# Attention output with tokens on partitions: the state's part on two row groups, masked scores as full weights

## The chip, the cores and the metric

The kernel runs on one core of a Trainium2 chip. The metric is the device time of one execution in microseconds, the median over several runs. A ratio is the mean time of one kernel's fast runs over the mean time of the other's fast runs of the same rounds, so it is not quite the ratio of the medians that are quoted.

## The reference

A block-wise linear attention ("lightning attention") is followed by a mixer. There are 4 batches, 8 heads, 768 tokens and 64 channels per head; all is float32.

```python
for b in range(nb):                                   # blocks along the tokens
    intra = einsum('bhic,bhjc->bhij', qb, kb) * Dmask
    intra = einsum('bhij,bhjd->bhid', intra, vb)
    inter = einsum('bhid,bhde->bhie', qb * lam_pow, kv_state)
    out[:, :, sl] = intra + inter
    kv_state = lam_block * kv_state + einsum('bhsd,bhse->bhde', kb * rev_pow, vb)
# x = out as (batch, token, head*channel)
u  = x + (x^T @ U @ V)^T                              # low rank over the tokens, rank 32
out = u + relu(u @ w_ch1) @ w_ch2                     # 512 -> 2048 -> 512
```

The kernel uses blocks of 128 tokens, 6 per batch, so it goes through 24 blocks (`s` = 0 to 23), each for all 8 heads. Head `h = 2a + x` has `a` from 0 to 3 and `x` 0 or 1; `x` chooses the upper or the lower 64 partitions.

## The kernel before

Only the attention front is concerned. In each block, q and k are transposed (`prep`), the scores are formed and masked, and the output comes out with *channels* on partitions: v and the state are the weights, the masked scores and the queries are moved through. It is then transposed back.

```python
kv  = consts.tile([P, HP, P], FP32)      # state of two heads, block-diagonal, zeros between
kvc = consts.tile([P, HP, D], FP32)      # the same without the zeros

def outputs(s):
    px = bank([P, HP, P], "px", "a2")
    for a in range(HP):
        if c > 0:
            for x in range(2):
                rows = slice(x * D, (x + 1) * D)
                nc.tensor.matmul(out=px[rows, a, :], lhsT=kv[:, a, rows], rhs=qs[:, a, :], ...)   # L359
        for x in range(2):
            nc.tensor.matmul(out=px[x*D:(x+1)*D, a, :], lhsT=vr[:, 2*a+x, :], rhs=sm[:, x, a, :], ...)  # L364
    nc.scalar.copy(xt, px)
    state(s)

def state(s):                            # pkv = (scaled k)^T v, 8 matmuls, L380
    for a in range(HP):
        nc.vector.scalar_tensor_tensor(kvc[:, a, :], kvc[:, a, :], lamc[:, a, :], pkv[:, a, :], ALU.mult, ALU.add)
    for x in range(2):                   # into the block-diagonal form
        nc.scalar.copy(kv[d, :, d], kvc[d])

def back(s):                             # four transposes, L404
    for ct in range(CT):
        nc.tensor.transpose(out=px[:, ct, :], in_=xt[:, ct, :], identity=ident)
    nc.scalar.copy(xs[s]..., px)
```

Later steps of a block are `mix` (adds the low-rank part to x), `turn` (transposes x for the first large product), and "side work": pieces of the conversion of U, V and the first weights, spread over the blocks.

## Time and profile before

| | before |
|---|---|
| median | 699.68 us (698.73 to 700.88, 4 runs) |
| span of the profiled run | 697.5 us |
| attention front, up to the first large product | 142.2 us |
| time per steady block | 5.67 us |

A steady block is one with everything in it: state, mix and turn. I measure a block from the start of its scores to the start of the next scores. The groups that the change touches, in the first 155 us (columns: line, engine, operation, output and inputs, shapes, count; busy us and mean ns of one; idle time before them):

```profile
L364 PE MATMUL px<-sm,vraw 128*64 128x128 f32 x384 | 35.4, 274 | 0.4 <-DVE x_nat L450 0.3
L359 PE MATMUL px<-qs,kv 128*64 128x128 f32 x320 | 32.1, 279 | 0.0
L364 PEld LDWEIGHTS px<-sm,vraw 128*64 128x64 f32 x384 | 23.6, 137 | 1.9 <-DVE x_nat L450 1.4 <-issue 0.4 <-DVE sm L347 0.2
L404 PE MATMUL pxn<-ident,xt 128*128 128x128 f32 x96 | 15.7, 286 | 0.4 <-ACT xt L369 0.4
```

`128*64 128x128` is a matmul with 128 rows and 64 columns of weights and 128 moving columns. The 384 instructions of L364 are 24 blocks x 8 heads x 2, because each float32 product stands in the trace as two instructions, each with its own weight load. The mean of 274 ns is one instruction's latency. Many overlap, so pace must be read from the chain, not from the mean.

### The profile page before, as it was taken

What the parts mean: (1) busy time and instruction counts of PE and PEld (TensorE: products, weight loads), DVE (VectorE), ACT (ScalarE), POOL (GpSimd) and SP (SyncE); (2) the same over time, 40 slices, a digit from 0 to 9 for tenths busy, and PEclk for the clock granted to TensorE, in tenths of its full rate; (3) what the DMA queues carried; (4) which work ended last, traced back from release to release, by engine and by line L of the source; (5) the groups of instructions that cost most, each with busy time, mean ns of one, the idle gap of its engine ahead of it and who ended that gap; (6) DMA issues with size and microseconds to landing.
All of it is one profiled execution on the core that took longest, in us unless ns stands there. A gap on an engine that the chain in (4) does not pass through costs nothing.

```text
span 697.5 us, 11418 instructions
## 1 busy us (share of the span) xinstructions
PE 685.6 (98%) x4194; PEld 556.0 (80%) x4194; DVE 502.0 (72%) x905; ACT 306.6 (44%) x543; POOL 108.0 (15%) x91
## 2 busy tenths in 40 slices
PE   7999999998999999999999999999999999999997
PEld 6879797976888888888888888888888888888886
DVE  5768687867899777777779436778577586775864
ACT  4767777844566544444455322232232222322320
POOL 4425554523000000000000000011030030300300
PEclk9999999999999999999999999999999999999999
DMA  9977686224476565556557889966344363352521
GB/s 219 228 182 183 167 221 163 90 81 168 173 256 245 197 210 210 208 209 208 205 206 266 296 304 359 341 206 200 98 153 155 91 211 103 120 185 91 166 92 60
DMA packets 131530, 131.17 MB, mean 188 GB/s; under 512 B 81234, under 2 KB 89426, under 8 KB 131474
## 3 DMA queue, kind: packets, MB, share of 16 engines
q1 hardware_dynamic: 129376, 129.92, 57.8%
q10 hardware_dynamic: 2098, 0.52, 0.3%
q8 instruction: 33, 0.54, 0.3%
q14 instruction: 23, 0.19, 0.1%
HBM read 80.09 MB, written 50.33 MB: 187 GB/s over the span
## 4 chain that ended last, share of the span: by engine, by line
PE 93%; DVE 4%; issue 1%; ACT 1%; DMA 1%; ACTq 0%; DVEq 0%
PE pz L638 25%; PE pz L771 13%; PE pz L769 13%; PE pd L773 13%; PE pd L648 12%; PE pss L341 3%; PE px L364 3%; PE px L359 2%; PE pxn L404 2%; PE pkv L380 2%; PE put L464 1%; PE pk L306 1%; PE pq L306 1%; DVE ut L469 1%; DVE sm L347 1%; PE pr L433 1%
## 5 line engine op out<-in xcount | busy, mean ns | idle before, releaser
L638 PE MATMUL pz<-u_hl,w 128*128 128x512 f32 x768 | 190.6, 398 | 1.1 <-ACT uf L476 1.1
L638 PEld LDWEIGHTS pz<-u_hl,w 128*128 128x128 f32 x768 | 144.4, 188 | 37.1 <-ACT uf L476 1.5
L771 PE MATMUL pz<-w_hl,m 128*128 128x512 f32 x384 | 151.6, 396 | 0.0
L769 PE MATMUL pz<-w_hl,m 128*128 128x512 f32 x384 | 151.6, 396 | 0.0
L773 PE MATMUL pd<-w_d,m 128*128 128x512 f32 x384 | 150.0, 396 | 0.0
L752 ACT ACTIVATE m<-mt 128x512 fp32r<-128x512 f32 x96 | 60.7, 632 | 196.8 <-PE pd L773 137.0
L753 DVE SCALAR_TENSOR_TENSOR m<-rm,m 128x512 fp32r<-128x512 f32 x96 | 71.5, 746 | 52.3 <-ACT m L752 52.1
L653 DVE SCALAR_TENSOR_TENSOR r<-pd,r 128x512 f32<-128x512 f32 x96 | 61.8, 686 | 57.2 <-ACT r L644 47.2
L793 POOL TENSOR_TENSOR o<-o,u 128x512 f32<-128x512 f32 x20 | 29.8, 1522 | 452.1 <-DVE o L791 452.1
L648 PE MATMUL pd<-u_d,w 128*128 128x512 f32 x384 | 98.8, 397 | 0.0
L769 PEld LDWEIGHTS pz<-w_hl,m 128*128 128x128 f32 x384 | 72.3, 188 | 17.7
L771 PEld LDWEIGHTS pz<-w_hl,m 128*128 128x128 f32 x384 | 72.3, 188 | 17.6
L773 PEld LDWEIGHTS pd<-w_d,m 128*128 128x128 f32 x384 | 72.3, 188 | 17.6
L648 PEld LDWEIGHTS pd<-u_d,w 128*128 128x128 f32 x384 | 72.2, 188 | 17.4
L644 ACT ACTIVATE r<-pz 128x512 f32<-128x512 f32 x96 | 51.9, 593 | 62.4 <-PE pz L638 62.4
L754 DVE SCALAR_TENSOR_TENSOR m<-m 128x512 fp32r<-128x512 f32 x96 | 69.1, 721 | 0.9
L751 DVE TENSOR_SCALAR mt<-rm 128x512 uint32<-128x512 uint32 x96 | 46.2, 482 | 28.2 <-DMA rm<-r_d 27.6
L347 DVE TENSOR_TENSOR sm<-pss,mask 128x512 f32<-128x512 f32 x48 | 30.9, 686 | 11.5 <-PE pss L341 9.3
L179 ACT CAST w<-wt 128x512 fp32r<-128x512 f32 x32 | 19.9, 622 | 41.8 <-DVE wt L176 33.5
L364 PE MATMUL px<-sm,vraw 128*64 128x128 f32 x384 | 35.4, 274 | 0.4 <-DVE x_nat L450 0.3
L359 PE MATMUL px<-qs,kv 128*64 128x128 f32 x320 | 32.1, 279 | 0.0
L136 ACT ACTIVATE sc<-sc,ends 128x512 f32<-128x512 uint32 x29 | 21.0, 723 | 19.2 <-DVE sc L132 19.2
(88 smaller groups left out, 761.9 us busy)
## 6 DMA issues: line engine op xcount, KB each, us to landing
r_d<-r SPq DMA_DIRECT2D x96, 256.0 KB, 2.7
rm<-r_d SPq DMA_DIRECT2D x96, 256.0 KB, 2.6
words<-in_moe_w_ch_dram SPq DMA_DIRECT2D x32, 512.0 KB, 4.4
w_d<-w SPq DMA_DIRECT2D x16, 768.0 KB, 3.3
w_hl<-w_d SPq DMA_DIRECT2D x16, 512.0 KB, 6.0
u_d<-x_nat SPq DMA_DIRECT2D x24, 256.0 KB, 3.0
u<-u_d SPq DMA_DIRECT2D x24, 256.0 KB, 4.3
out_dram<-o SPq DMA_DIRECT2D x24, 256.0 KB, 2.0
```

The lines of the kernel that those rows point to most:

```text
L364: nc.tensor.matmul(out=px[x * D : (x + 1) * D, a, :], lhsT=vr[:, 2 * a + x, :], rhs=sm[:, x, a, :], start=(c == 0), stop=True,)
L638: nc.tensor.matmul(out=acc[g][0], lhsT=w[:, n, ct, :], rhs=uhl[g][:, n, ct, :], start=(ct == 0 and n == 0), stop=(ct == CT - 1 and n == 1),)
L644: nc.scalar.mul(rs[g], acc[g][0], 1.0 + E)
L648: nc.tensor.matmul(out=acc[g][1], lhsT=w[:, 2, ct, :], rhs=ud[g][:, ct, :], start=(ct == 0), stop=(ct == CT - 1),)
L653: nc.vector.scalar_tensor_tensor(rs[g], acc[g][1], 4096.0, rs[g], ALU.mult, ALU.add)
L751: nc.vector.tensor_scalar(t.bitcast(U32), r.bitcast(U32), HI, None, ALU.bitwise_and)
L752: nc.scalar.activation(out=m[:, 0], in_=t, func=AF.Relu)
L753: nc.vector.scalar_tensor_tensor(m[:, 1], r, 0.0, hi, ALU.max, ALU.subtract)
L754: nc.vector.scalar_tensor_tensor(m[:, 2], hi, E, low, ALU.mult, ALU.subtract)
L769: nc.tensor.matmul(out=pz, lhsT=m[:, 0, cols], rhs=hl[:, 0], start=first, stop=False)
L771: nc.tensor.matmul(out=pz, lhsT=m[:, 1, cols], rhs=hl[:, 1], start=False, stop=end)
L773: nc.tensor.matmul(out=pd, lhsT=m[:, 2, cols], rhs=dd, start=first, stop=end)
```

## The change

It intends to get x straight with *tokens* on partitions, so that the transposes back and a copy go away. For that the roles are swapped: queries and masked scores become the weights, the state and v move. The state's part uses two row groups (64 rows each), so the state needs no zero blocks; its fading by lambda goes to ScalarE; PSUM is laid out anew for the front, with pairs of banks for scores and output; the order of the steps is changed.

```diff
-    kv = consts.tile([P, HP, P], FP32, name="kv")
-    kvc = consts.tile([P, HP, D], FP32, name="kvc")
+    def fade(s):
+        if 0 < s % NT < NT - 1:
+            for a in range(HP):
+                nc.scalar.mul(faded[:, a, :], kv[s][:, a, :], lamc[:, a, :])
     def state(s):
+            if c == 0:
+                nc.vector.tensor_copy(out=kv[s + 1], in_=pkv)
+            else:
+                nc.vector.tensor_tensor(out=kv[s + 1], in0=pkv, in1=st[s]["faded"], op=ALU.add)
-    def back(s): ...            # four transposes and the loop of outputs(s) go
+    def inter(s):
+        for a in range(HP):
+            for x in range(2):
+                nc.tensor.matmul(
+                    out=px[:, x, a, :], lhsT=st[s]["qs"][half[x], a, :], rhs=kv[s][half[x], a, :],
+                    start=(a == 0), stop=False,
+                )
+    def intra(s):
+        for a in range(HP):
+            for x in range(2):
+                nc.tensor.matmul(
+                    out=px[:, x, a, :], lhsT=sm[:, x, a, :], rhs=vr[:, 2 * a + x, :],
+                    start=first, stop=(first or a == HP - 1),
+                )
+        nc.scalar.copy(xs[s].rearrange("p (a x e) -> p x a e", a=HP, x=2), px)
...
-        step += [("scale", s + 1)] + [("aside", s)] + [("mix", done)] + [("low", b - 1)]
-        step += [("outputs", s)] + [("low_sum", b - 1)] + [("scores", s + 1), ("back", s)] + [("turn", done)]
+        step = [("prep", s + 1), ("fade", s), ("scale", s + 1)] + [("mix", done)] + [("low", b - 1)]
+        step += [("intra", s)] + [("turned", done - 1)] + [("aside", s)] + [("low_sum", b - 1)]
+        step += [("state", s)] + [("scores", s + 1), ("inter", s + 1)] + [("turn", done)]
+    pieces += [("mix", NS - NT - 1)]      # the last mix of the front, before: at the head of the first product's list
```

More of the change, by code (lines that the diff above doesn't have):

```diff
@@ L210, with two_banks, one_bank @@
     words_pool.append(att_ctx.enter_context(tc.tile_pool(name="words_a", bufs=1)))
-    ps = ctx.enter_context(tc.tile_pool(name="ps", bufs=8, space=bass.MemoryType.PSUM))
+    front_ctx = ctx.enter_context(ExitStack())
+    psf = front_ctx.enter_context(tc.tile_pool(name="psf", bufs=1, space=bass.MemoryType.PSUM))
+    def two_banks(name, tag):
+        return psf.tile([P, 2, N], FP32, tag=tag, name=name)
+    def one_bank(shape, name, tag):
+        return psf.tile(shape, FP32, tag=tag, name=name)
+    psa = []
     def bank(shape, name, tag):
-        return ps.tile(shape, FP32, tag=tag, bufs=2, name=name)
+        return psa[0].tile(shape, FP32, tag=tag, bufs=2, name=name)
     lamb = consts.tile([P, H], FP32, name="lamb")
@@ L272, in constants @@
         nc.vector.tensor_copy(out=rev, in_=mask[:, :, :, P - 1])
-        nc.gpsimd.memset(kv, 0.0)
     def powers():
@@ L297 @@
     st = {}
+    kv = {}
+    half = [slice(0, D), slice(D, P)]
     def prep(s):
@@ L302, in prep @@
         for a0 in range(0, HP, n):
-            for name, dst in (("q", qt), ("k", kt)):
-                pt = bank([P, n, P], "p" + name, "b2")
+            for name, dst, tag in (("q", qt, "pt" if a0 else "pq"), ("k", kt, "pu" if a0 else "pk")):
+                pt = one_bank([P, n, P], "p" + name, tag)
                 for a in range(a0, a0 + n):
@@ L332, in scale @@
             scale_k(s + 1)
+    def fade(s):
+        if 0 < s % NT < NT - 1:
+            st[s]["faded"] = faded = att.tile([P, HP, D], FP32, tag="faded", name="faded")
+            for a in range(HP):
+                nc.scalar.mul(faded[:, a, :], kv[s][:, a, :], lamc[:, a, :])
     def scores(s):
         qt, kt = st[s]["qt"], st[s]["kt"]
-        pss = [bank([P, HP, P], "pss", "a1") for x in range(2)]
+        pss = two_banks("pss", "pss").rearrange("p x (a i) -> p x a i", a=HP)
         for a in range(HP):
             for x in range(2):
-                rows = slice(x * D, (x + 1) * D)
                 nc.tensor.matmul(
-                    out=pss[x][:, a, :], lhsT=kt[rows, a, :], rhs=qt[rows, a, :],
+                    out=pss[:, x, a, :], lhsT=kt[half[x], a, :], rhs=qt[half[x], a, :],
                     start=True, stop=True,
@@ L346, in scores @@
         for x in range(2):
-            nc.vector.tensor_tensor(out=sm[:, x], in0=pss[x], in1=mask[:, x], op=ALU.mult)
+            nc.vector.tensor_tensor(out=sm[:, x], in0=pss[:, x], in1=mask[:, x], op=ALU.mult)
         st[s]["sm"] = sm
-    def outputs(s):
-        b, c = divmod(s, NT)
-        qs, sm, vr = st[s].get("qs"), st[s]["sm"], raw[s, "v"]
-        px = bank([P, HP, P], "px", "a2")
-        for a in range(HP):
-            if c > 0:
-                for x in range(2):
-                    rows = slice(x * D, (x + 1) * D)
-                    nc.tensor.matmul(
-                        out=px[rows, a, :], lhsT=kv[:, a, rows], rhs=qs[:, a, :],
-                        start=True, stop=False,
-                    )
-            for x in range(2):
-                nc.tensor.matmul(
-                    out=px[x * D : (x + 1) * D, a, :], lhsT=vr[:, 2 * a + x, :],
-                    rhs=sm[:, x, a, :], start=(c == 0), stop=True,
-                )
-        xt = att.tile([P, HP, P], FP32, tag="xt", bufs=1, name="xt")
-        nc.scalar.copy(xt, px)
-        state(s)
-        st[s] = xt
     def state(s):
-        b, c = divmod(s, NT)
+        c = s % NT
         if c < NT - 1:
             ks, vr = st[s]["ks"], raw[s, "v"]
-            pkv = bank([P, HP, D], "pkv", "a2")
+            pkv = one_bank([P, HP, D], "pkv", "pu")
             for a in range(HP):
@@ L380, in state @@
                     nc.tensor.matmul(
-                        out=pkv[x * D : (x + 1) * D, a, :], lhsT=ks[:, a, x, :],
-                        rhs=vr[:, 2 * a + x, :], start=True, stop=True,
-                    )
-            for a in range(HP):
-                if c == 0:
-                    if a == 0:
-                        nc.vector.tensor_copy(out=kvc, in_=pkv)
-                else:
-                    nc.vector.scalar_tensor_tensor(
-                        kvc[:, a, :], kvc[:, a, :], lamc[:, a, :], pkv[:, a, :],
-                        ALU.mult, ALU.add,
-                    )
@@ L393, in state @@
-            for x in range(2):
-                d = slice(x * D, (x + 1) * D)
-                nc.scalar.copy(kv[d, :, d], kvc[d])
+                        out=pkv[half[x], a, :], lhsT=ks[:, a, x, :], rhs=vr[:, 2 * a + x, :],
+                        start=True, stop=True,
+                    )
+            kv[s + 1] = att.tile([P, HP, D], FP32, tag="kv", bufs=2, name="kv")
+            if c == 0:
+                nc.vector.tensor_copy(out=kv[s + 1], in_=pkv)
+            else:
+                nc.vector.tensor_tensor(out=kv[s + 1], in0=pkv, in1=st[s]["faded"], op=ALU.add)
@@ L396, in state @@
+        del st[s]
         del raw[s, "v"]
         load_next("v")
-    def back(s):
-        xt = st.pop(s)
-        px = bank([P, CT, P], "pxn", "b1")
-        for ct in range(CT):
-            nc.tensor.transpose(out=px[:, ct, :], in_=xt[:, ct, :], identity=ident)
+    def inter(s):
+        st[s]["px"] = both = two_banks("px", "px")
+        px = both[:, :, 0 : HP * D].rearrange("p x (a e) -> p x a e", a=HP)
+        if s % NT == 0:
+            return
+        for a in range(HP):
[4 more added lines that the diff above has]
+                )
@@ L405, in back @@
+    def intra(s):
+        first = s % NT == 0
+        sm, vr, px = st[s]["sm"], raw[s, "v"], st[s]["px"]
+        px = px[:, :, 0 : HP * D].rearrange("p x (a e) -> p x a e", a=HP)
+        for a in range(HP):
[4 more added lines that the diff above has]
+                )
         xs[s] = x_pool.tile([P, C], FP32, tag="x", name="x_nat")
-        nc.scalar.copy(xs[s].rearrange("p (c n) -> p c n", n=P), px)
+        nc.scalar.copy(xs[s].rearrange("p (a x e) -> p x a e", a=HP, x=2), px)
@@ L409 @@
     pts = {}
     def low(b):
-        pp = bank([P, C], "pp", "a2" if b < B - 1 else "b2")
+        pp = two_banks("pp", "pss")[:, 0] if b < B - 1 else bank([P, C], "pp", "b2")
         for c in range(G):
@@ L418, in low @@
             )
-        half = C // 2
+        n = C // 2
         assert 2 * (NT - G) == G
         for i in range(G):
-            c, cols = G + i // 2, slice(i % 2 * half, (i % 2 + 1) * half)
+            c, cols = G + i // 2, slice(i % 2 * n, (i % 2 + 1) * n)
             nc.tensor.matmul(
@@ L431, in low_sum @@
     def low_sum(b):
-        pr = bank([P, C], "pr", "b1" if b < B - 1 else "b2")
+        pr = one_bank([P, C], "pr", "pt") if b < B - 1 else bank([P, C], "pr", "b2")
         nc.tensor.matmul(
@@ L445, in mix @@
         b, c = divmod(s, NT)
-        pu = bank([P, C], "pu", "a2" if s < NS - NT - 1 else "b2")
+        pu = one_bank([P, C], "pu", "pu") if s < NS - NT else bank([P, C], "pu", "b2")
         nc.tensor.matmul(
@@ L461, in turn @@
         cols = slice(n * P, (n + 1) * P)
-        pt = bank([P, CT, P], "put", "b1")
+        pt = one_bank([P, CT, P], "put", "pt") if g < FG else bank([P, CT, P], "put", "b1")
         for ct in range(CT):
@@ L488, in turn @@
         turned[s] = rest
-    pieces = [("prep", 0), ("scale", 0), ("scores", 0)]
+    pieces = [("prep", 0), ("scale", 0), ("scores", 0), ("inter", 0)]
     for s in range(NS):
@@ L497 @@
         done = s - NT - 1
-        step = [("prep", s + 1)] * (s + 1 < NS)
-        step += [("turned", done - 1)] * (done > 0)
-        step += [("scale", s + 1)] * (s + 1 < NS)
-        step += [("aside", s)]
+        more = s + 1 < NS
+        step = [("prep", s + 1)] * more + [("fade", s), ("scale", s + 1)] * more
         step += [("mix", done)] * (done >= 0)
         step += [("low", b - 1)] * (c == 0 and b > 0)
-        step += [("outputs", s)]
+        step += [("intra", s)] + [("turned", done - 1)] * (done > 0) + [("aside", s)]
         step += [("low_sum", b - 1)] * (c == 0 and b > 0)
-        step += [("scores", s + 1), ("back", s)] * (s + 1 < NS)
+        step += [("state", s)] + [("scores", s + 1), ("inter", s + 1)] * more
         step += [("turn", done)] * (done >= 0 and done // TG < FG)
         pieces += step
+    pieces += [("mix", NS - NT - 1)]
     waiting = {name: list(range(NS)) for name in "qkv"}
@@ L516 @@
     run = {
-        "prep": prep, "scores": scores, "outputs": outputs, "back": back,
+        "prep": prep, "fade": fade, "scores": scores, "inter": inter, "intra": intra,
+        "state": state,
         "low": low, "low_sum": low_sum, "mix": mix, "turn": turn,
@@ L591 @@
     make_gather()
-    pl = bank([P, H], "pl", "a2")
+    pl = one_bank([P, H], "pl", "pu")
     nc.tensor.matmul(out=pl, lhsT=lam_row[:, H:], rhs=lam_row[:, 0:H], start=True, stop=True)
@@ L596 @@
     scale_k(0)
+    powers()
     run["aside"] = aside
@@ L599 @@
         run[what](s)
-        if (what, s) == ("scores", 0):
-            powers()
     assert not side
+    front_ctx.close()
+    psa.append(
+        ctx.enter_context(
+            tc.tile_pool(name="ps", bufs=2, space=bass.MemoryType.PSUM, reuse_waits="tile")
+        )
+    )
     def enter_first_product(s):
@@ L692 @@
     rest = [
-        (0, 0, "mix", c0 - 1), (0, 4, "back", NS - 1), (0, 4, "enter", None),
+        (0, 4, "enter", None),
         (0, 4, "turn", c0 - 2), (0, 9, "low", b), (0, 14, "low_sum", b),
```

## The prediction

> **What bounds the kernel now.** I read the page first (busy shares and the chain that ended last), then the table of windows, the chain of one steady attention block, the groups of instructions, and single rows of the timeline. The page:
>
> ```profile
> PE 685.6 (98%) x4194; PEld 556.0 (80%) x4194; DVE 502.0 (72%) x905; ACT 306.6 (44%) x543; POOL 108.0 (15%) x91
> ...
> PE 93%; DVE 4%; issue 1%; ACT 1%; DMA 1%; ACTq 0%; DVEq 0%
> PE pz L638 25%; PE pz L771 13%; PE pz L769 13%; PE pd L773 13%; PE pd L648 12%; PE pss L341 3%; PE px L364 3%; PE px L359 2%; PE pxn L404 2%; PE pkv L380 2%; PE put L464 1%; PE pk L306 1%; PE pq L306 1%; DVE ut L469 1%; DVE sm L347 1%; PE pr L433 1%
> ```
>
> TensorE carries 93% of the chain. Three quarters of the span (the products of lines 638 to 773) are not touched. Only the attention front, about the first 142 us, changes. There, too, TensorE hardly rests, while VectorE and ScalarE are busy about 75% (columns: stretch, length, then busy us and count for PE, PEld, DVE, ACT, POOL, then clock, DMA share, GB/s):
>
> ```profile
> 80.00:100.00 20.00, 19.81 (x270) 17.59 (x270) 16.80 (x37) 16.10 (x31) 9.55 (x8) 1.00 0.74 194
> 100.00:120.00 20.00, 19.66 (x261) 16.05 (x259) 14.91 (x28) 14.49 (x28) 9.70 (x9) 1.00 0.72 180
> ```
>
> Busy time alone could hide waits, so I took one steady block from the chain (start, us, work):
>
> ```profile
> 90.03 0.56 PE pkv L380 x16
> 90.59 1.09 PE pss L341 x16
> 91.68 0.59 PE pxn L404 x4
> 92.27 0.44 PE put L464 x4
> 92.70 0.44 PE pq L306 x4
> 93.14 0.44 PE pk L306 x4
> 93.58 0.23 PE pu L447
> 93.81 0.37 PE px L359 x4
> 94.18 0.22 PE px L364 x4
> 94.39 0.22 PE px L359 x4
> ...
> 95.70 0.63 PE pkv L380 x16
> ```
>
> The block lasts 95.70 - 90.03 = 5.67 us and every piece of it is TensorE. So freed work on VectorE or ScalarE is worth nothing here; what counts is whether TensorE's own list of work gets longer or shorter. The chain shows 4.91 us for each early block (no residual mix, no turning yet) and 71.26 to 84.91 for two blocks, one of which carries the low-rank sums: those contain VectorE pieces, but the timeline has TensorE idle for only some 0.6 us before px there, so there is little waiting to win back.
>
> **What the Trainium skill says, and whether the trace agrees.** (1) "TensorE: Matmul & The Clock Gate", section "LDWEIGHTS (loading the stationary operand)": a weight load takes its number of columns / 1.2 ns, whatever the number of rows: 107 ns for 128 columns, 53 for 64. The trace agrees where two full fp32 loads stand back to back:
>
> ```profile
> 77.69 0.30 PEld L433 LDWEIGHTS pr<-pt,gather 128*128 128x128 f32 x2
> 77.69 1.12 PE L433 MATMUL pr<-pt,gather 128*128 128x512 f32 x2
> ```
>
> One load lasts 188 ns (its mean in the groups), two end after 0.30 us, so the second began some 0.11 us after the first. (2) "TensorEngine Tiling (Array Packing)", "Key Properties": tiles run in parallel, and changing the tiling mode drains the engine. The trace agrees: in px, four instructions on two column tiles take 0.22 us, a pair per 0.109, while the first four after the switch take 0.37. (3) The same page, "Gotcha 1: PSUM Pressure": row tiles write different banks; the change gives x two banks, as the scores have already. (4) "ScalarE: Activation LUTs", "What ACT_TABLE_LOAD costs": an activation is 186 ns + 0.833 ns per element, 93 more for a per-partition operand. The 64x256 copy kv should then take 399 ns; the trace has 404.
>
> What sets a matmul's pace in this kernel: each fp32 product is two instructions[...]. A group streams at the larger of its weight load (columns x 0.84 ns) and its moving side (128 columns per 109 ns, from the transposes: 0.44 us for four), since loads run ahead of running matmuls. pkv: 64 against 64 columns on two column tiles, 0.56 us for eight pairs. px: 64 weight columns against 128 moving, eight pairs 0.88 us. pss: 128 against 128 on two row tiles, 1.09 with the fill, 0.112 per pair.
>
> **The change part by part**, in a steady block.
> - The transposes back go: pxn, -0.59 us of TensorE, and one ScalarE copy of 0.58 (xt). x is then written by one strided copy of 0.6, as now.
> - px from state and queries (L359) becomes "inter": queries are the weights, 64 rows x 128 columns, on two row tiles; the state moves, 64 columns. The moving side halves, but the weight side doubles, so the load sets the pace as in pss: 8 pairs x 0.112 = 0.90 us, against 8 x 0.109 = 0.87 now. It follows pss in the same mode, so no drain between. About even: the zeros that are left out gave nothing, because the two column tiles already ran side by side.
> - px from masked scores and v (L364) becomes "intra": 128x128 weights with 64 moving columns, no tiling. Before: 8 pairs x 0.109 = 0.87. After: 16 single instructions, one after the other, each paced by a 128-column load: 16 x 0.109 = 1.75 us. This is +0.88, more than the transposes give back.
> - Fill and drain: px's first-four excess of 0.15 goes; inter's end before put and intra's end before pkv add 0.05 and 0.10. About even.
> - VectorE: four kvc updates of 276 ns (1.10) become one 128x256 add, some 0.42 as the copy kvc<-pkv takes: -0.68, off the path. ScalarE: two kv copies (0.81) and xt (0.58) go; four fades come, each 280 + 53 = 333 ns by the skill's formula, 0.24 apart, 1.0 in all: -0.4, off the path.
>
> New steady block: pkv 0.56 + pss 1.09 + inter 0.90 + put 0.49 + pq 0.44 + pk 0.44 + pu 0.23 + intra 1.85 = 6.00, against 5.67: +0.33.
>
> Over the front of 24 blocks: nine steady ones x 0.33 = 3.0; three that follow a low-rank block (5.8 to 6.1 now, with waits, 6.0 after) +0.2; the four early ones 4.91 less pxn 0.59 and px 1.85, plus 0.90 and 1.85 and a pkv that no longer starts in px's mode (0.1): +0.4 each, 1.6; the last of a batch, no state update, two x 0.3 = 0.6; the one at 31 us loses 0.1, since its wait for the side work (VectorE vt, 1.3 us, ahead of ScalarE xt) falls away when side work moves behind intra; the three with low-rank sums have no inter and lose their waits, -0.15 together; the very first has no pxn to lose, +0.8. Sum 5.95. At the end the moved mix (VectorE add 0.68 and its latencies) holds the bank that the first product wants: +0.8, an estimate; the last transposes back (0.44) go, but the last inter and intra cost as much more. So 699.8 + 6 = some 706 us.
>
> **The rivals.**
> (a) The matmul is bound by what moves, not by loads, as the change's author may think: intra would be 16 x 0.055 = 0.87, inter 0.45; a block loses 0.59 + 0.45, some 24 us in all, 676 to 680. Against: pr's loads 0.11 apart; nothing in the trace has a 128-column load with 64 moving columns, so it isn't directly seen.
> (b) Load and stream don't overlap on the full array: intra 16 x (0.107 + 0.055) = 2.6 us, +0.85 a block, 725 us. Against: put and pq run four 128-column transposes at 0.109 each with their loads inside, and the untouched fp32r products have 188 ns loads under a 233 ns pace. But their moving side is the longer one; a switch cost of 10 to 17 ns per instruction when the load is the longer is possible and adds up to 6 us (712).
> (c) New waits: x's two banks, pkv, put's bank have one buffer each now. inter(s+1) needs the x copy of s (intra's end + 0.8; pkv and pss give 1.65) and the state's add (pkv's end + 0.6, pss gives 1.0). VectorE's list per block is then some 4.6 us of 6.0. These fit, except in the low-rank blocks (VectorE has 5.9 us there), where a few tenths could be lost: 707 to 709.
> (d) The shorter dependency saves hidden waits: at most the 0.2 to 0.4 us of the eight irregular blocks, 2 to 3 us: 703.
>
> **Range and chances.** The centre is 706. (c), (d) and a switch cost give -4 to +6: 701 to 712 should hold it 8 times in 10. Over 2% slower needs 713.8, a pace of 0.13 us in intra or waits in each block: 0.12. Over 2% faster needs 685.8, nearly all of (a): 0.05. Within 2%: 0.83.
>
> **What would show it.** intra's 16 instructions in about 1.75 us (0.109 apart) and inter's in about 0.9 to 1.0; PEld busy longer per block; pss starts 6.0 us apart instead of 5.67 in steady blocks, 5.3 instead of 4.91 early; VectorE and ScalarE with more idle time that nobody uses; the products after 142 us at the same pace, merely shifted by 6 us. I am wrong if intra takes 0.9 us (rival a), over 2 us (b), or if TensorE waits for the x copy or the state's add in most blocks (c).

## The result, and the profile after

The changed kernel takes 710.0 us (708.83 to 710.58, 4 runs), against 699.68: ratio 1.0144, interval 1.0124 to 1.0165. It is 1.4% slower, which is within 2%, as the prediction gave most chance to, and within the predicted 701 to 712. But the change of time was +10.3 us, not +6.2, so 4 us are to be explained beside the right mechanism. (Three of the four runs, the profiled one among them, have a slightly lower mean clock, of which more below; the one with a mean clock of 1.000 took 708.83 us.)

The page of the changed kernel, the same lines as in the prediction:

```profile
PE 694.8 (98%) x4098; PEld 571.2 (81%) x4098; DVE 500.5 (71%) x857; ACT 291.3 (41%) x543; POOL 108.4 (15%) x90
...
PE 95%; DVE 3%; ACT 1%; issue 0%; DMA 0%; ACTq 0%; DVEq 0%
PE pz L647 25%; PE pz L780 13%; PE pz L778 13%; PE pd L782 13%; PE pd L657 12%; PE px L405 6%; PE pss L356 3%; PE px L394 3%; PE put L468 2%; PE pq L316 2%; PE pk L316 2%; PE pkv L372 1%; DVE ut L473 1%; PE pu L451 1%; PE pp L419 1%; PE pr L437 1%
```

TensorE has 96 instructions fewer (the transposes back) and is busy 9.2 us longer; PEld grew by 15.2. VectorE and ScalarE both have less to do, and the time went up all the same. In the chain, px from the masked scores (L405) has doubled its share, from 3% to 6%. One steady block of the chain:

```profile
64.28 0.61 PE pkv L372 x16
64.90 1.09 PE pss L356 x16
65.99 0.84 PE px L394 x16
66.83 0.59 PE put L468 x4
67.42 0.44 PE pq L316 x4
...
68.29 0.23 PE pu L451
68.52 1.73 PE px L405 x16
70.25 0.62 PE pkv L372 x16
```

It lasts 70.25 - 64.28 = 5.97 us, and all of it is TensorE, as before. Intra (L405) is 1.73, where the eight pairs of L364 took 0.88. The groups show what changed in it:

```profile
L405 PEld LDWEIGHTS px<-vraw,sm 128*128 128x128 f32 x384 | 46.0, 192 | 1.9 <-issue 1.2
L405 PE MATMUL px<-vraw,sm 128*128 128x64 f32 x384 | 45.9, 272 | 0.0
L394 PEld LDWEIGHTS px<-kv,qs 64*128 64x128 f32 x320 | 19.6, 188 | 2.9 <-POOL ks L329 1.5 <-issue 1.4
L349 ACT ACTIVATE faded<-kv,powq 128x64 f32<-128x64 f32 x64 | 17.1, 347 | 0.0
```

For L405 the weight loads are busy as long as the matmuls, 46 us; before, L364 had 23.6 us of loads beside 35.4 of matmuls. The single starts in the trace agree: loads begin 112 ns apart, and each matmul 55 ns after its load. What is not in this view is which of the two, load or stream, sets those 112 ns. The first experiment asks that.

**Where the 11.0 us of the two spans are.** From the starts of the scores in both traces, and, for the end, the starts of the first large product:

| stretch | before us | after us | change | predicted |
|---|---|---|---|---|
| start to the first scores | 6.71 | 6.05 | -0.66 | 0 |
| the first block | 5.09 | 5.79 | +0.70 | +0.8 |
| four early blocks | 19.64 | 22.67 | +3.03 | +1.6 |
| the block at 31 us | 4.91 | 4.69 | -0.22 | -0.1 |
| nine steady blocks | 51.2 | 53.7 | +2.5 | +3.0 |
| two last of a batch | 10.24 | 10.71 | +0.47 | +0.6 |
| three with low-rank sums | 21.98 | 22.87 | +0.89 | -0.15 |
| the three after those | 17.80 | 19.34 | +1.54 | +0.2 |
| last scores to the first product | 4.60 | 6.04 | +1.44 | +0.8 |
| first 20 matmuls of the product | 10.53 | 11.80 | +1.27 | 0 |

The start differs by when the first k landed (the load takes 3.61 us in one trace, 3.23 in the other); runs of the changed kernel and its variants have it anywhere from 6.0 to 6.95, so it is no effect of the change. (The predicted column sums to 6.75; the prediction added 6.) The rows where the prediction missed are the early blocks, the low-rank blocks and those after them, and the end. TensorE's waits in the changed kernel's front lie there (what waited, for whom; us in total, times, longest):

```profile
PE px L394 <- DVE kv L380: 1.2, 1, 1.2
PE px L394 <- DVE kv L378: 1.1, 3, 0.4
PE pz L647 <- DVE ends L81: 0.8, 1, 0.8
PE pp L419 <- DVE sm L362: 0.5, 1, 0.5
PE pu L451 <- DVE x_nat L454: 0.2, 1, 0.2
```

The first is the block at 22 us, the second the three blocks after a low-rank sum, the fourth the first low-rank block (at 40 us), the other two the end. Behind such a wait inter also takes 1.11 us in the chain instead of 0.84.

*The early blocks.* Three take 5.30, as predicted; the one at 22 us takes 6.77. Its chain:

```profile
20.17 1.75 PE px L405 x16
...
21.94 0.59 ACT x_nat L410
22.53 0.36 ACT sc L136
...
23.40 0.55 DVE sc L153
...
24.25 0.43 DVE kv L380
...
24.81 1.11 PE px L394 x16
```

The chain leaves TensorE. Side work (the conversion of U, lines 136 to 158) stands behind the copy of x on ScalarE and ahead of the state's add on VectorE. VectorE takes its list in order here: the products that the add (L380) needs end at 22.5 us, but it starts only at 24.25, behind the side work, and inter starts at 24.81, behind the add. So the add waits for two ScalarE steps that have nothing to do with it.

*The blocks after the low-rank sums.* There the copy that begins the new batch's state (L378) stands behind two VectorE steps of the low-rank sum (`pt_h`, `vp`), and inter waits 0.4 us in each of the three.

*The end.* The moved mix starts only when VectorE has added the mix ahead of it, and the first product only when the moved mix is added too. Between the two adds VectorE has 0.6 us of side work. I read this as one bank that all three use; the trace shows the waits, not the bank. In the profiled run a slow clock follows (columns: stretch, length; busy us and count for PE, PEld, DVE, ACT, POOL; granted clock, DMA share, GB/s):

```profile
150.00:155.00 5.00, 4.00 (x15) 2.96 (x15) 2.03 (x6) 1.64 (x3) 1.27 (x1) 0.70 0.28 105
155.00:160.00 5.00, 5.00 (x30) 2.72 (x29) 1.20 (x2) 1.80 (x3) 1.28 (x1) 0.96 0.00 0
```

A clock of 0.70 over 5 us and 0.96 over the next is (0.30 + 0.04) x 5 = 1.7 us lost, which is 3.4 us at half speed. The first four matmuls of the product show it: 1.97 us here, 1.20 in a variant (`e9_u_spread`, below) that has the same wait before them and no slow clock:

```profile
151.88 1.97 PE L647 MATMUL pz<-u_hl,w 128*128 128x512 f32 x4 [0.78 <-DVE ends L81]
150.87 1.20 PE L647 MATMUL pz<-u_hl,w 128*128 128x512 f32 x4 [0.78 <-DVE ends L81]
```

In all six variants below that keep this end, the first 20 matmuls take 10.21 to 10.22 us. So the slow clock cost 11.80 - 10.22 = 1.58 us, more than the 1.27 of the table: the stretch had become 0.31 us shorter, presumably as the last transposes back no longer stand in it. The end without the slow clock is thus +1.44 - 0.31 = +1.1 us, against +0.8 predicted.

The Trainium skill, "TensorE: Matmul & The Clock Gate", Part 1 ("The HAM clock gate"), says that the clock falls to half after an idle window of about 3.4 us and recovers after a busy one, with a window that runs freely. The length of the slow stretch agrees. The cause agrees only loosely: the timeline has TensorE idle for 1.0 us ahead of the product (0.22 us before the last mix, 0.78 after it), not for a whole window. The drop is not in every run either: of the changed kernel's four, the mean clock was 0.998, 0.999, 0.998 and 1.000, with 710.28, 709.72, 710.58 and 708.83 us.

### The profile page after: what moved, and what is told of

The parts are those of the page before. It is cut to its first block, busy times and chain, and to the rows that moved or that the text cites. A ratio compares the mean times of both kernels' runs of the same rounds, so it can differ in the third digit from the quotient of the medians.

```text
span 708.5 us, 11107 instructions
## 1 busy us (share of the span) xinstructions
PE 694.8 (98%) x4098; PEld 571.2 (81%) x4098; DVE 500.5 (71%) x857; ACT 291.3 (41%) x543; POOL 108.4 (15%) x90
## 4 chain that ended last, share of the span: by engine, by line
PE 95%; DVE 3%; ACT 1%; issue 0%; DMA 0%; ACTq 0%; DVEq 0%
PE pz L647 25%; PE pz L780 13%; PE pz L778 13%; PE pd L782 13%; PE pd L657 12%; PE px L405 6%; PE pss L356 3%; PE px L394 3%; PE put L468 2%; PE pq L316 2%; PE pk L316 2%; PE pkv L372 1%; DVE ut L473 1%; PE pu L451 1%; PE pp L419 1%; PE pr L437 1%
## 5 line engine op out<-in xcount | busy, mean ns | idle before, releaser
L405 PEld LDWEIGHTS px<-vraw,sm 128*128 128x128 f32 x384 | 46.0, 192 | 1.9 <-issue 1.2
L405 PE MATMUL px<-vraw,sm 128*128 128x64 f32 x384 | 45.9, 272 | 0.0
L362 DVE TENSOR_TENSOR sm<-pss,mask 128x512 f32<-128x512 f32 x48 | 30.9, 686 | 15.2 <-PE pss L356 15.0
L320 ACT COPY qt<-pq 128x512 f32<-128x512 f32 (+1 forms) x25 | 14.2, 569 | 42.6 <-PE pq L316 42.6
```

What stands on the lines that cost most here:

```text
L405: nc.tensor.matmul(out=px[:, x, a, :], lhsT=sm[:, x, a, :], rhs=vr[:, 2 * a + x, :], start=first, stop=(first or a == HP - 1),)
```

## The experiments

Theory W: TensorE's own list of work sets the time, and in the new products the 128-column weight load sets the pace, at about 0.11 us per load, with the stream hidden under it. Its rivals are that the stream sets the pace, that load and stream add up, or that 0.112 us is a fixed cost of an instruction. Theory Q: the missing 4 us are, beside the slow clock, waits on VectorE's and ScalarE's lists in four or five places, not in the steady blocks. All kernels gave correct results; each is an edit of the changed kernel.

**Double the stream, keep the loads.** The same 64 columns are streamed twice, the second copy into unused columns of the bank.

```diff
-   out=px[:, x, a, :], lhsT=sm[:, x, a, :], rhs=vr[:, 2*a+x, :]
+   out=px[:, x, a, :, :], lhsT=sm[:, x, a, :], rhs=vr[:, 2*a+x : 2*a+x+1, :].broadcast_to([P, 2, D])
-   out=px[:, x, a, :], lhsT=qs[half[x], a, :], rhs=kv[half[x], a, :]
+   out=px[:, x, a, :, :], lhsT=qs[half[x], a, :], rhs=kv[half[x], a : a+1, :].broadcast_to([D, 2, D])
```

> The changed kernel with the moving side of both new products doubled: the same 64 columns of v and of the state are streamed twice (128 columns), the weights unchanged. Theory W (the 128-column weight load sets the pace, streams hide under it): intra stays at 0.11 us per instruction, inter at 0.11 per pair, the time stays at 710 within 2 us (ratio to the kernel before 1.012 to 1.018). Rival M (the stream sets the pace, or load and stream add up): intra goes from 0.11 to about 0.165 us per instruction, +0.85 us a block, inter up to +0.45, so 730 to 740 us.

Measured: 711.24 us (710.85 to 711.73, 4 runs), ratio 1.0170 (1.0156 to 1.0184). The chain of this kernel:

```profile
67.39 0.89 PE px L394 x16
...
69.98 1.78 PE px L406 x16
```

Twice the stream costs 0.05 us in each product, once per block, which fits the longer last stream (55 ns more); the other fifteen instructions hide it. Sixteen streams of 0.109 us fit into 1.78 us. So with 64 columns the stream does not set the pace, and load and stream do not add up. Rival M is out; the load, or a fixed cost of an instruction, is left.

**Halve the load: intra on two column tiles.** Each 128x128 weight is cut into two of 64 columns (64 query tokens each), which go to different column halves of the array.

```diff
+   for t in half:
-       out=px[:, x, a, :], lhsT=sm[:, x, a, :], rhs=vr[:, 2*a+x, :]
+       out=px[t, x, a, :], lhsT=sm[:, x, a, t], rhs=vr[:, 2*a+x, :]
```

> The changed kernel with each masked-score product cut into two, 64 query tokens (weight columns) each, on two column tiles: 32 instructions of 64 weight columns and 64 moving ones instead of 16 of 128 and 64. Theory W (load sets the pace, loads of two tiles run side by side, as in pkv at 0.058 per pair): intra falls from 1.73 to about 0.93 us, -0.8 a block, 24 blocks: about 691 us, ratio 0.987, though waits on VectorE may keep back some us. Rival F (0.112 is a fixed cost per instruction, whatever its load): 16 pairs at 0.112, no gain, 710 or more.

Measured: 696.97 us (696.3 to 697.29, 4 runs), ratio 0.9964 (0.9951 to 0.9978). That is 13 us faster than the changed kernel, and a little faster than the kernel before. The chain and the loads:

```profile
64.87 1.08 PE px L406 x32
```

```profile
L406 PEld LDWEIGHTS px<-vraw,sm 128*64 128x64 f32 x768 | 25.3, 142 | 6.2 <-DVE ut L474 3.1 <-issue 2.1 <-DMA vraw<-in_v_dram 0.4
```

Twice as many instructions do the same arithmetic in 1.08 us instead of 1.73: two half-size loads run side by side, as the prediction had seen in pkv. This settles intra against rival F. (The edit changes the tiling mode along with the width of the weights; the next run does so where both forms are tiled, with the same outcome.) My expectation of 691 us was too low by 6. The gain of a steady block is 0.6 to 0.66 us (5.31 to 5.38 against 5.97), not 0.8, presumably since fill and mode switch remain; and the block at 22 us got longer, 7.92 us instead of 6.77, because TensorE came to the same wait earlier, idled longer (1.6 us instead of 1.2), and then had a stretch of half clock (0.66 from 25 to 30 us).

**Halve the loads of both products.** Inter is cut as well, into four tiles of 64 rows and 64 columns.

```diff
+   for t in half:
-       out=px[:, x, a, :], lhsT=qs[half[x], a, :], rhs=kv[half[x], a, :]
+       out=px[t, x, a, :], lhsT=qs[half[x], a, t], rhs=kv[half[x], a, :]
```

> As the run with split masked scores (697 us), and the state's part cut in the same way: queries of 64 tokens, 64 rows x 64 columns of weights, four tiles. Theory W4 (four tiles load and stream side by side): inter's 32 instructions take 0.46 to 0.6 us instead of 0.94 with its fill, -0.35 to -0.45 us in 20 blocks, about 689 us. Rival P (instructions start in order and each product is two of them on one tile, so only two run at a time): 16 pairs x 0.058 = 0.93 us, no gain, 697 us.

Measured: 689.67 us (688.67 to 691.54, 4 runs), ratio 0.9862 (0.9834 to 0.989). In the chain:

```profile
79.42 0.62 PE px L395 x32
...
81.74 1.08 PE px L407 x32
```

Inter falls from 0.84 to 0.62 us with twice the instructions, so four tiles do work side by side. The time fits the expectation, but partly by luck: the scores lose 0.10 us per block, presumably since inter no longer shares their tiling mode (from their start to the next product they take 1.092 us instead of 0.995), so a steady block gains 0.21 us and 20 blocks some 4 us. Most of the other 3 us are the block at 22 us (5.98 instead of 7.92, without the slow clock), the first block (4.90 instead of 5.87) and the start. The first block holds no inter, so its gain is no effect of the cut.

**Fading back on VectorE.** The state is updated as before the change, by four VectorE instructions, and ScalarE fades nothing.

```diff
-   nc.vector.tensor_tensor(out=kv[s+1], in0=pkv, in1=st[s]["faded"], op=ALU.add)
+   for a in range(HP):
+       nc.vector.scalar_tensor_tensor(kv[s+1][:, a, :], kv[s][:, a, :], lamc[:, a, :], pkv[:, a, :], ALU.mult, ALU.add)
```

> The changed kernel with the old way of updating the state: four VectorE instructions per block (0.28 us each) instead of four fades on ScalarE and one add of 0.42. Theory T (TensorE's list of work decides; VectorE's spare time is worth nothing): the state is ready some 0.45 us later, 0.38 us of that fits under the scores, so 710 to 712 us (ratio 1.014 to 1.018). Rival: the fade is what holds the new order together, without it each inter waits half a us: 718 us or more.

Measured: 709.67 us (708.58 to 710.41, 4 runs), ratio 1.0139 (1.0118 to 1.016): the same as the changed kernel within the noise. Steady blocks stay at 5.97. So in this kernel the part "fading on ScalarE" is worth nothing either way; it moves work between two engines that both have time.

**The waits, one at a time.** First, the state ahead of the low-rank sum, and the side work behind the next scores and inter:

```diff
-   intra, turned, aside, low_sum, state, scores, inter, turn
+   intra, turned, state, low_sum, scores, inter, aside, turn
```

> The changed kernel with the state's update ahead of the low-rank sum, and the side work behind the next block's scores and inter. Theory Q (VectorE takes its list in order, so the state's add waits behind side work and inter waits for it): the 6.77 us block at 22 us goes back to 5.3, the two blocks of 6.59 to about 6.1, together -2.4 us: 707.5, ratio 1.0108. Rival: the waits only move to the scores' masks or to the turning, and the time stays at 710 (ratio 1.0144).

Measured: 710.43 us (708.9 to 711.6, 5 runs), ratio 1.0157 (1.0141 to 1.0173). The block at 22 us does go from 6.77 to 5.31, and two of the blocks after a low-rank sum from 6.59 to 5.97 and 6.04. But the block that stands as "at 31 us" in the table goes from 4.69 to 6.05, those with low-rank sums from 7.67 to 7.81, three other stretches grow by 0.3 to 0.4: the rival was right about the time, the waits moved. But the longest of the new ones is not where it put them: the scores wait 0.9 us for a copy of the keys on ScalarE, behind side work. (The first block of this profile, 6.71 us instead of 5.79, is set apart: its eight transposes took 1.89 us instead of 1.29, as in three profiles with other edits.) Here an order that freed one engine's list at one point loaded it at another.

Second, only the piece that stood in the way: two of the four pieces of U's conversion one block earlier.

```diff
-   (u_side, (-1, 2, 2, 2, 2)),
+   (u_side, (-1, 1, 1, 2, 2)),
```

> The changed kernel with two of the four pieces of the conversion of U done one block earlier, nothing else. Theory Q (the 1.5 us that the block at 22 us waits are one chain of side work, ScalarE then VectorE, ahead of the state's add): that block goes from 6.77 to 5.3 to 5.4 us, no other block gains as much, and the time falls by 1.2 to 1.5 us, to about 708.6 (ratio 1.0125). Rival: the wait moves to the block before or after it and the time stays at 710 (1.0144).

Measured: 708.54 us (707.67 to 708.8, 4 runs), ratio 1.0125 (1.0111 to 1.0139). The block at 22 us takes 5.31, all later blocks stay within 0.01 us of what they were, and the wait of inter for the add is gone from the trace. Theory Q holds for this wait, with 1.5 us in its block. The gain in time is less sure: this profile's first block is 0.44 us longer (its eight transposes took 1.88 us instead of 1.29), and all four runs had a mean clock of 1.0, so that part of the 1.5 us between the medians is the slow clock of the changed kernel, whose one undisturbed run took 708.83.

Third, the end: the last mix inside the first product again, now behind its fourth matmul (in the kernel before it ran just ahead of the first).

```diff
-   pieces += [("mix", NS - NT - 1)]
+   (0, 4, "mix", c0 - 1),          # in the list of what runs inside the first product
```

> The changed kernel with the last mix of the front put back into the first product (behind its fourth matmul), so that the first product doesn't wait for VectorE's add to give its bank free. Theory H (TensorE's 1.4 us of idle at 150 us, and the slower clock that follows it, cost the last 2.7 us of the 10.9): about 707.3 us, ratio 1.0105, with no stretch of slow matmuls at 152 us. Rival: another bank (that of x) holds the product back as long, 709 to 710 us.

Measured: 708.5 us (707.79 to 709.14, 4 runs), ratio 1.0130 (1.0116 to 1.0144). From the last scores to the first product it takes 4.77 us instead of 6.04, close to the 4.60 of the kernel before, and the next 20 matmuls take 10.45, the mix among them. That is 15.22 us together, against 6.04 + 10.22 = 16.26 for the same end without a slow clock: 1.0 us gained. All four runs had a mean clock of 1.0. The times give 1.5 us by the medians, 1.0 by the ratios (0.0014 x 699), whose intervals overlap; the medians again mix in the slow clock, and the 2.7 us that I expected counted it as if every run had it. The run with the new order kept the idle time at the end, and its profile has no slow clock there (1.00 from 150 to 160 us); the run with U's pieces moved kept it too, and all four of its runs had a mean clock of 1.0. So the same idle time is followed by the drop in some runs and not in others.

**Together.** Both splits with the mix put back:

> Both splits and only the last mix inside the first product: 1 to 1.5 us under the run with both splits.

Measured: 688.47 us (687.48 to 689.68, 4 runs), ratio 0.9838 (0.9815 to 0.9861). That is 1.2 us under both splits alone; the intervals of the ratios overlap, but the traces agree (4.55 + 10.44 us at the end instead of 5.84 + 10.22).

Both splits, the mix, and a milder new order (state, low-rank sum, side work, then scores):

> Both splits, the last mix inside the first product, and the state's update ahead of the low-rank sum and of the side work, the side work ahead of the next scores. If the waits that the prediction missed can be had back: 1.5 to 3 us from the block at 22 us (its long idle time also cost a slow clock in the split run), 1 us from the blocks behind the low-rank sums, 1 from the handover: 3 to 5 us under the run with both splits alone. If they only move, no more than 1 us under it.

Measured: 693.32 us (692.81 to 693.74, 4 runs), ratio 0.9906 (0.9888 to 0.9925), some 5 us *over* the same kernel without the new order. Its waits (engine, what waited, for whom; us in total, times, longest):

```profile
PE pkv L372 <- DVE x_nat L456: 3.6, 7, 0.9
PE px L407 <- DVE sm L362: 3.2, 6, 1.0
```

With the side work ahead of the masks, intra waits for its masked scores and pkv for its bank. These two waits are absent without the new order. It may be that a shorter list on TensorE leaves VectorE's order less room; this order was not run without the splits.

Last, both splits, the mix put back and U's pieces one block earlier:

> Both splits, the last mix inside the first product, and the pieces of U one block earlier: 1.3 to 1.7 us under the same without the last (688.5), about 687 us, ratio 0.982.

Measured: 687.34 us (686.26 to 687.98, 5 runs), ratio 0.9824 (0.9811 to 0.9838). It is 1.1 us under the run without U's pieces moved, less than expected, and the intervals overlap; in the trace the block that waited goes from 5.97 to 4.29 us, the one after it from 4.29 to 4.61. This beats both kernels: 1.8% faster than the one before, and 3.2% faster than the changed one (687.34 / 710.0 = 0.968).

## Why the prediction was right or wrong

- *TensorE's list sets the time; VectorE's and ScalarE's spare time is worth nothing.* Right for the steady blocks: both engines had less to do, and the block grew from 5.67 to 5.97 us. The run with fading back on VectorE shows it once more.
- *The transposes back go, 0.59 us.* Right.
- *Inter is about even, 0.90 us.* Right: 0.84 plus its drain, 0.94 from its start to the next.
- *Intra takes 1.75 us, paced by 128-column loads.* Right: 1.73, at 0.112 per load instead of 0.109. Shown from both sides, by doubling the stream (+0.05 us) and by splitting the load (-0.65 us). The load time of 107 ns that the prediction takes from the skill fits the pace of the loads; a single load is recorded with 192 ns.
- *A steady block 6.00 us.* 5.97. The nine steady blocks gave +2.5 instead of +3.0.
- *Range and chances.* 710.0 lies inside 701 to 712, and "within 2%" came true. The centre was 4 us low, and the change itself was forecast at 6.2 against 10.3. Of this, 0.75 us is a slip: the prediction's terms are 5.95 and 0.8, and it added 6.
- *The step that was mis-sized is (c), the new waits.* It said that they fit, "except in the low-rank blocks", where "a few tenths could be lost". The runs showed 1.5 us in one early block, some 2.4 us in the low-rank blocks and those behind them (+0.89 and +1.54 where the sum had -0.15 and +0.2), and at the end 0.3 us more than the 0.8 estimated. The profiled run also has 1.58 us of slow clock, which no term of the prediction held.
- *Why it failed.* I set VectorE's work of a mean block (4.6 us) against the block's length, and did not read the order of its list at each special block. The moved side work was counted only where it helped, at 31 us (-0.1 forecast, -0.22 measured). The same move put U's conversion ahead of the state's add two blocks earlier. The early rows had each block at +0.4, which three of them kept.
- *Rival (d)*, that irregular blocks would win back their waits, was wrong in sign: the low-rank blocks and those behind them grew by 2.4 us together; only the one at 31 us won back 0.2.

What stays open: why the block with low-rank sums at 40 us grew by 0.7 us. Its chain shows the low-rank sum waiting for the masks that hold its bank, and I did not test another bank for it. What starts the slow clock is open too. Nor did I undo single parts in the other direction, within the kernel before.

## What to carry to other kernels

Before swapping what stands and what moves, compute both sides of each matmul: here a group went at the larger of its weight load (0.112 us for 128 columns) and its stream (0.109 us for 128 columns), and a stream of 64 columns (0.055 us) was hidden under a full load. If weights with 128 columns must meet 64 moving ones, cut the weights into 64-column tiles, so that two or four loads run side by side; here that turned a change that lost 10 us into one that wins nearly 10, and 12 with two of the waits removed. And where steps are reordered, read the list of each engine in the irregular blocks: averages hide a wait that one foreign instruction at the wrong place makes.

## What the Trainium skill lacked or had wrong

- "TensorE: Matmul & The Clock Gate", Part 3, says under "What overlaps and what doesn't" that a weight load overlaps with running matmuls only when the row group differs, though the paragraph before it allows for a background buffer. Here intra uses the full array throughout, and doubling its stream from 64 to 128 columns left sixteen load-and-matmul pairs at 1.78 us instead of 1.73. So they overlap on the same rows too.
- The same page gives the time of a weight load, and "TensorEngine Tiling (Array Packing)" says that tiles load in parallel, but the latter advises column tiling only for weights of 64 columns or fewer, and for a short moving side to swap the two sides, which is how the kernel before stands. It lacks that a full 128-column weight is worth cutting when the stream is short: 16 instructions in 1.73 us became 32 in 1.08, and on four tiles 16 in 0.84 became 32 in 0.62.
- "TensorE: Matmul & The Clock Gate", Part 1, asks for an idle window of about 3.4 us before the clock falls. Here it fell after two idle pieces of 0.22 and 0.78 us at the end of the front, in the profile of the changed kernel and not in those of six variants with the same end, and the slow clock then cost 1.6 us in the first 20 matmuls. (The same part also tells of short idling between groups of matmuls that brings the clock down, but gives no length for it.)
